# RWKV-7 attention before a mixture of experts: products over the head dimension issued for both head parities in turn

## The chip, the cores and the metric

The kernel runs on one core of one Trainium2 chip. The metric is the device time of one execution in microseconds (us). Three runs of the kernel before gave 2517.96, 2530.65 and 2545.3 us; the median is 2530.65 us.

The engines that matter here are TensorE (PE; its weight loads are listed apart as PEld), VectorE (DVE) and ScalarE (ACT), which empty PSUM, GpSimd (POOL), and SyncE (SP), which starts most transfers. Every matrix product is in float32. The profile shows one such product as two weight loads and two matmuls.

## The reference

The first part is a linear attention with a state per head, 4 batch rows, 8 heads, 768 steps, head dimension 40:

```
for t in range(S):
    y[:, :, t] = einsum('bhd,bhde->bhe', rt, state)
    Sa = einsum('bhde,bhe->bhd', state, at)
    state = state * wt[..., None, :] - einsum('bhd,bhe->bhde', Sa, bt)
    state = state + einsum('bhd,bhe->bhde', vt, kt)
```

Its output, as 3072 rows of 320, goes through a top-1 mixture of 8 experts (320 to 1024 to 320, a relu between), each row scaled by its gate weight.

## The kernel before, in words

The attention is cut into chunks of 128 steps: 6 chunks for each of 4 batch rows, 24 units, taken chunk by chunk (units 0 to 3 are the first chunk and have no incoming state). A unit holds all 8 heads as 4 head pairs. The even head of a pair (parity 0) has its 40 dimensions on partitions 0 to 39, the odd head (parity 1) on partitions 64 to 103; `rows(par)` is that slice. So a product over the head dimension reads 40 partitions of one half, and a product over time reads all 128.

Each unit is done by four functions.

- `prepare` loads the inputs, forms the running product of w, its reciprocal (DVE) and the scaled inputs, and transposes four tensors (`ps_nat`, 16 transposes).
- `systems` builds, for each parity, four masked 128x128 matrices per head by products over the head dimension (`ps_GT`, `ps_NT`, `ps_N`, `ps_AT`, line 177, 40 rows), and then squares the system matrix: 9 sets of four products over time (`ps_NT`, `ps_N`, line 177, 128 rows), emptied by ACT.
- `attend` solves the system for each parity: a right side (`ps_r`: for each head pair a product with the state, line 224, 40 rows, then one with `GT`, line 225, 128 rows), 8 sets of four products (`ps_q`, line 216), each set waiting for the DVE addition of the one before. Then come the transposes of the solution (`ps_uT`, line 246), the masked products `ps_ZT` (line 177, 40 rows), the output `ps_y` (for each head pair lines 263, 264 and 267: 40, 128 and 128 rows), the new state (`ps_s`, lines 273 and 274, written to one column half) and its transpose (`ps_st`, line 284).
- `route` computes the logits (`ps_xT`, `ps_lg`) and stores the gated rows.

The loop prepares unit u+1 and builds its systems, then attends to unit u, so the squaring of one unit and the chain of `ps_q` of another can share TensorE. PSUM has two rings: `big`, 5 buffers of 2 KB a partition, and `small`, 3. The order in each engine's queue is fixed when the program is built: a scheduler places the instructions, and every engine then works down its own list and waits where a result is missing.

The second part routes the rows and runs the experts; the change does not touch it.

Of the kernel before, what the change touches and what calls it, by code (L numbers as in the profile page):

```python
# [8 lines left out]
F32 = mybir.dt.float32  # L9
# [7 lines left out]
# Order of the six tensors in the packed attention input.  # L17
# [4 lines left out]
def kernel(  # L22
# [20 lines left out]
    N = B * S  # L43
# [10 lines left out]
    # The model dimension in contraction blocks.  # L54
# [3 lines left out]
    # Routing: NJ blocks of 128 rows for each expert, the rest in NX blocks shared by all.  # L58
# [50 lines left out]
    # Token numbers as float16 holds them: 1.. for the first half, -1.. for the second.  # L109
# [15 lines left out]
    with tc.tile_pool(name="ring", bufs=1) as ring, \  # L125
# [3 lines left out]
        # Head 2p+par has its dims at partitions par*64...; the partitions between hold harmless values.  # L129
# [24 lines left out]
        def prepare(u):  # L154
# [10 lines left out]
            # The same by time on the partitions.  # L165
# [18 lines left out]

        def systems(d):
            I = d["I"]
            for par in range(2):
                def of(n, par=par):
                    return lambda p: I[rows(par), n, p, :]

                def mat(t):
                    return lambda p: t[:, p, :]
# [14 lines left out]
        def attend(u, d):  # L207
# [10 lines left out]

            for par in range(2):
                rs = rows(par)  # L220
                q = small("ps_r")
                for p in range(NP):
                    if c:
                        nc.tensor.matmul(q[:, p, :], lhsT=I[rs, A, p, :], rhs=ST[rs, p, :], start=True, stop=False)  # L224
                    nc.tensor.matmul(  # L225
                        q[:, p, :], lhsT=d["GT", par][:, p, :], rhs=nV[:, p, par, :D], start=(c == 0), stop=True,
                    )
                X = sb.tile([C, NP, D], F32, name="X", bufs=6)
                nc.scalar.copy(X[:], q[:])
# [25 lines left out]
            for par in range(2):  # L255
                rs = rows(par)
                ZT = product(
                    lambda p: uT[rs, p, :], lambda p: I[rs, R, p, :], before, "ZT", 2,
                )
                q = small("ps_y")  # L260
                for p in range(NP):
                    if c:
                        nc.tensor.matmul(q[:, p, :], lhsT=I[rs, R, p, :], rhs=Sn[rs, p, :], start=True, stop=False)  # L263
# [6 lines left out]
                if c + 1 < NCH:  # L270
# [12 lines left out]
                    for p in range(NP):  # L283
                        nc.tensor.matmul(q[rs, p, :], lhsT=STn[rs, p, :], rhs=ident[rs, rs], start=True, stop=True)  # L284
# [285 lines left out]
```

## Time and profile before

| | |
|---|---|
| runs | 2517.96, 2530.65, 2545.3 us (median 2530.65) |
| profiled execution | span 2515.5 us, mean granted TensorE clock 0.716 |
| TensorE busy | 2373.8 us (94%), weight loads 2069.5 us (82%) |
| VectorE, ScalarE, GpSimd busy | 529.6 us, 415.7 us, 151.8 us |
| transfers | 59.58 MB, mean 24 GB/s |
| first part of the kernel (16 to 2135 us) | clock 0.98 up to 103 us, 0.72 up to 331 us, 0.66 up to 2051 us |
| experts (2200 to 2515 us) | clock 0.99 |

The page's busy times count an engine as busy while any of its instructions is under way. The granted clock of TensorE stands at one of two levels, 0.50 (1.2 GHz) or 1.00 (2.4 GHz); a figure between is a stretch with both. The time of the profiled execution is known by its span; what lies around the span is not listed, and the fastest of the three runs is 2.5 us above it.

### The profile page before, as it was taken

To read this page: it belongs to the slowest core of one execution; us is meant where nothing else is said; L and a number is where in the kernel's file an instruction comes from. 1 tells how busy PE (TensorE), PEld (TensorE's weight loads), DVE (VectorE), ACT (ScalarE), POOL (GpSimd) and SP (SyncE) were. 2 spreads that over 40 slices of the span, in tenths; PEclk is the share of its full clock that TensorE was granted. 3 is DMA by queue.
4 is the path that set the end of the run, shared out by engine and by line. 5 is a ranking of instruction groups with operands and counts; after the bars stand their busy time and mean duration, and the time that the engine had idled before them with its cause. 6 is when DMAs were issued, how large, how long until landed. Compare 5 with 4: busy or idle time off the path is not lost.

```text
span 2515.5 us, 29177 instructions
## 1 busy us (share of the span) xinstructions
PE 2373.8 (94%) x12916; PEld 2069.5 (82%) x12916; DVE 529.6 (21%) x1157; ACT 415.7 (17%) x849; POOL 151.8 (6%) x185
## 2 busy tenths in 40 slices
PE   6999999999999999999999999999999998699998
PEld 5999988998898898898899899899889887244544
DVE  2212222122122122122212112213112111311110
ACT  1312211221121121121121121111112110001010
POOL 4000000000000000000000000000000000311101
PEclk9877657766765766666676676676677665799999
DMA  1000000000000000000000000000000000522210
GB/s 48 19 9 11 19 19 16 4 19 19 1 19 19 3 17 19 10 10 19 16 3 19 16 4 19 19 1 19 19 1 19 3 1 3 155 93 85 86 51 16
DMA packets 20560, 59.58 MB, mean 24 GB/s; under 512 B 2893, under 2 KB 14159, under 8 KB 18512
## 3 DMA queue, kind: packets, MB, share of 16 engines
q1 hardware_dynamic: 16992, 48.50, 6.6%
q0 software_dynamic: 3072, 9.18, 1.2%
q8 instruction: 102, 1.67, 0.3%
q14 instruction: 26, 0.21, 0.0%
q10 hardware_dynamic: 368, 0.01, 0.0%
HBM read 49.82 MB, written 9.18 MB: 23 GB/s over the span
## 4 chain that ended last, share of the span: by engine, by line
PE 82%; issue 11%; DVE 3%; POOL 2%; ACT 1%; DMA 0%; POOLq 0%; DVEq 0%; ACTq 0%
PE ps_q L216 20%; PE ps_NT L177 14%; PE ps_N L177 11%; PE ps_y L264 4%; PE ps_ZT L177 4%; PE ps_y L267 4%; PE ps_y L263 3%; PE ps_nat L169 3%; PE ps_r L225 3%; PE ps_r L224 3%; PE ps_AT L177 3%; PE ps_GT L177 3%; DVE X L233 2%; POOL out_dram L493 1%; PE ps_st L284 1%
## 5 line engine op out<-in xcount | busy, mean ns | idle before, releaser
L216 PE MATMUL ps_q<-X,NT 128*128 128x40 f32 x2304 | 399.7, 332 | 52.7 <-DVE X L233 50.2
L216 PEld LDWEIGHTS ps_q<-X,NT 128*128 128x128 f32 x2304 | 378.2, 248 | 70.1 <-DVE X L233 65.7
L177 PE MATMUL ps_NT<-NT,N 128*128 128x128 f32 x1920 | 332.6, 326 | 1.3 <-ACT N L180 1.0
L177 PEld LDWEIGHTS ps_NT<-NT,N 128*128 128x128 f32 x1920 | 282.6, 226 | 13.2 <-issue 8.9
L177 PE MATMUL ps_N<-N,NT 128*128 128x128 f32 x1536 | 249.7, 317 | 0.0
L180 ACT COPY NT<-ps_NT 128x512 f32<-128x512 f32 x240 | 140.4, 585 | 584.9 <-PE ps_NT L177 584.9
L177 PEld LDWEIGHTS ps_N<-N,NT 128*128 128x128 f32 x1536 | 235.2, 234 | 0.0
L233 DVE TENSOR_TENSOR X<-ps_q,X 128x160 f32<-128x160 f32 x240 | 77.6, 323 | 574.9 <-PE ps_q L216 574.9
L474 PE MATMUL hp<-xgT,w 128*128 128x512 f32 (+1 forms) x384 | 190.9, 627 | 0.0
L474 PEld LDWEIGHTS hp<-xgT,w 128*128 128x128 f32 (+1 forms) x384 | 63.2, 189 | 122.4 <-issue 120.4
L216 PE MATMUL ps_q<-Z,NT 128*128 128x40 f32 x768 | 142.1, 348 | 20.5 <-DVE Z L242 20.5
L216 PEld LDWEIGHTS ps_q<-Z,NT 128*128 128x128 f32 x768 | 135.8, 266 | 27.7 <-DVE Z L242 27.7
L487 PE MATMUL zp<-w,h_sb 128*128 128x320 f32 x512 | 145.0, 433 | 0.0
L180 ACT COPY N<-ps_N 128x512 f32<-128x512 f32 x192 | 112.3, 585 | 107.9 <-PE ps_N L177 107.9
L264 PE MATMUL ps_y<-natK,AT 128*128 128x40 f32 x384 | 123.0, 420 | 0.0
L487 PEld LDWEIGHTS zp<-w,h_sb 128*128 128x128 f32 x512 | 94.6, 191 | 34.5 <-issue 0.8
L267 PE MATMUL ps_y<-natB,ZT 128*128 128x40 f32 x384 | 120.1, 415 | 0.0
L267 PEld LDWEIGHTS ps_y<-natB,ZT 128*128 128x128 f32 x384 | 101.9, 327 | 6.8 <-issue 4.3
L264 PEld LDWEIGHTS ps_y<-natK,AT 128*128 128x128 f32 x384 | 96.4, 311 | 13.3 <-issue 0.9
L177 PE MATMUL ps_ZT<-in,uT 40*128 40x128 f32 x384 | 101.0, 440 | 4.6 <-ACT uT L248 2.7
L263 PE MATMUL ps_y<-S,in 40*128 40x40 f32 x320 | 100.9, 414 | 0.0
L158 POOL MEMSET PT<- 128x4 f32 x24 | 2.5, 105 | 1573.8 <-DVE ST L279 1280.2
(150 smaller groups left out, 2384.4 us busy)
## 6 DMA issues: line engine op xcount, KB each, us to landing
in<-in_packed_dram SPq DMA_DIRECT2D x48, 480.0 KB
w<-in_moe_w_dram SPq DMA_DIRECT2D x8, 1280.0 KB
w<-in_moe_w_dram SPq DMA_DIRECT2D x8, 1024.0 KB
x_rows<-xs SPq DMA_DIRECT2D x24, 160.0 KB
w<-in_moe_w_dram SPq DMA_DIRECT2D x8, 256.0 KB
xg<-x_rows,g_idx POOLq DMA_INDIRECT x32
out_dram<-zo,s_idx POOLq DMA_INDIRECT x32
wg_sb<-in_moe_w_gate_dram ACTq DMA_DIRECT2D x2, 4.0 KB
```

What stands on the lines that cost most here:

```text
L169: nc.tensor.transpose(ps[:, p, :], src[:, p, :], ident[:])
L177: nc.tensor.matmul(ps[:, p, :], lhsT=lhs(p), rhs=rhs(p), start=True, stop=True)
L180: nc.scalar.copy(t[:], ps[:])
L216: nc.tensor.matmul(q[:, p, :], lhsT=m[:, p, :], rhs=x[:, p, :], start=True, stop=True)
L224: nc.tensor.matmul(q[:, p, :], lhsT=I[rs, A, p, :], rhs=ST[rs, p, :], start=True, stop=False)
L225: nc.tensor.matmul(q[:, p, :], lhsT=d["GT", par][:, p, :], rhs=nV[:, p, par, :D], start=(c == 0), stop=True,)
L233: nc.vector.tensor_tensor(Xn[:], q[:], X[:], op=ALU.add)
L263: nc.tensor.matmul(q[:, p, :], lhsT=I[rs, R, p, :], rhs=Sn[rs, p, :], start=True, stop=False)
L264: nc.tensor.matmul(q[:, p, :], lhsT=d["AT", par][:, p, :], rhs=nK[:, p, par, :D], start=(c == 0), stop=False,)
L267: nc.tensor.matmul(q[:, p, :], lhsT=ZT[:, p, :], rhs=nB[:, p, par, :D], start=False, stop=True)
L474: nc.tensor.matmul(hp[:, :cols], lhsT=g["w"][0][:dsz, db, fb * 128 : (fb + 1) * 128], rhs=g["xT"][:dsz, db, :cols], start=(db == 0), stop= ...
L487: nc.tensor.matmul(zp[:], lhsT=g["h"][:, fb, j * 128 : (j + 1) * 128], rhs=g["w"][1][:, fb, :], start=(fb == 0), stop=(fb == FB - 1),)
```

## The change

The four masked matrices of `systems` and the `ps_ZT` products are built by a new function, `twin`, which takes two PSUM buffers, one for each parity, and issues the products of the two parities in turn, pair by pair. All of `systems`' matrices of both parities are built before the squaring of either begins. The right side is made for both parities ahead of both chains: first the 8 products with the state, the parities in turn, then the 8 with `GT`. The new state is computed ahead of the output, with the parities in turn, and the output's 8 state products come as one group ahead of those with `AT` and `ZT`, which stay together by parity. No product is added or left out; the PSUM rings keep their sizes, and `ZT` has 4 buffers in place of 2.

```
+        def twin(lhs, rhs, mask, tag, bufs):
+            ps = [big(f"ps_{tag}") for _ in range(2)]
+            for p in range(NP):
+                for par in range(2):
+                    nc.tensor.matmul(ps[par][:, p, :], lhsT=lhs(par, p), rhs=rhs(par, p), start=True, stop=True)
+            ts = []
+            for par in range(2):
+                t = sb.tile([128, NP, 128], F32, name=tag, bufs=bufs)
+                nc.vector.tensor_tensor(t[:], ps[par][:], mask[:, None, :].to_broadcast([128, NP, 128]), op=ALU.mult)
+                ts.append(t)
+            return ts
...
+            d["GT"] = twin(of(K), of(A), before, "GT", 4)
+            NT0 = twin(of(B_), of(A), before, "NT0", 4)
+            N0 = twin(of(A), of(B_), after, "N", 4)
+            d["AT"] = twin(of(V), of(R), before, "AT", 4)
             for par in range(2):
-                d["GT", par] = product(of(K), of(A), before, "GT", 4)
-                NTk = product(of(B_), of(A), before, "NT0", 4)
-                Nk = product(of(A), of(B_), after, "N", 4)
-                d["AT", par] = product(of(V), of(R), before, "AT", 4)
+                NTk, Nk = NT0[par], N0[par]
...
+            qr = [small("ps_r") for _ in range(2)]
+            if c:
+                for p in range(NP):
+                    for par in range(2):
+                        rs = rows(par)
+                        nc.tensor.matmul(
+                            qr[par][:, p, :], lhsT=I[rs, A, p, :], rhs=ST[rs, p, :], start=(p == 0), stop=False,
+                            skip_group_check=True,
+                        )
+            for p in range(NP):
+                for par in range(2):
+                    nc.tensor.matmul(
+                        qr[par][:, p, :], lhsT=d["GT"][par][:, p, :], rhs=nV[:, p, par, :D],
+                        start=(c == 0 and p == 0), stop=True, skip_group_check=True,
+                    )
...
+            ZT = twin(lambda par, p: uT[rows(par), p, :], lambda par, p: I[rows(par), R, p, :], before, "ZT", 4)
...
+            qy = [small("ps_y") for _ in range(2)]
+            if c:
+                for p in range(NP):
+                    for par in range(2):
+                        rs = rows(par)
+                        nc.tensor.matmul(
+                            qy[par][:, p, :], lhsT=I[rs, R, p, :], rhs=Sn[rs, p, :], start=(p == 0), stop=False,
+                            skip_group_check=True,
+                        )
+            for par in range(2):
+                for p in range(NP):
+                    nc.tensor.matmul(
+                        qy[par][:, p, :], lhsT=d["AT"][par][:, p, :], rhs=nK[:, p, par, :D],
+                        start=(c == 0 and p == 0), stop=False, skip_group_check=True,
+                    )
+                    nc.tensor.matmul(
+                        qy[par][:, p, :], lhsT=ZT[par][:, p, :], rhs=nB[:, p, par, :D], start=False, stop=True,
+                        skip_group_check=True,
+                    )
```

The lists below are pieces of TensorE's queue in a unit of the middle of the kernel, one row for each run of equal products. `in_130` and `in_131` are input buffers of two successive units; names with a number are buffers.

First place: the start of `systems`. Before, the products of parity 0 alone:

```order
L177 MATMUL ps_GT<-in_131 128x128 x4
L177 MATMUL ps_NT_3587<-in_131 128x128 x4
L177 MATMUL ps_N<-in_131 128x128 x4
L177 MATMUL ps_AT<-in_131 128x128 x4
L177 MATMUL ps_NT_3608<-NT_3592,N 128x128 x4
L177 MATMUL ps_N<-N,NT_3592 128x128 x4
L216 MATMUL ps_q<-X,NT_3149 128x40 x4
```

With the change, in the same place:

```order
L190 MATMUL ps_GT<-in_131 128x128 x8
L190 MATMUL ps_NT_3587<-in_131 128x128
L190 MATMUL ps_NT_3588<-in_131 128x128
...
L190 MATMUL ps_N<-in_131 128x128 x8
L190 MATMUL ps_AT<-in_131 128x128 x8
L177 MATMUL ps_NT_3629<-NT_3597,N 128x128 x4
L177 MATMUL ps_N<-N,NT_3597 128x128 x4
L239 MATMUL ps_r<-ST_2055,in_130 128x40 x8
L245 MATMUL ps_r<-natV,GT 128x40
```

The rows with x8 alternate the parities as the `ps_NT` rows do. The four sets of parity 1, which stood between the squaring of parity 0 and that of parity 1, have moved up here, and `ps_r`, which stood ahead of the transposes and in the second squaring, has moved down.

Second place: the end of the squaring and the chain of `ps_q`. Before:

```order
L177 MATMUL ps_NT_3755<-NT_3746,N 128x128 x4
L216 MATMUL ps_q<-X,NT_3219 128x40 x4
L216 MATMUL ps_q<-X,NT_3240 128x40 x4
L216 MATMUL ps_q<-X,NT_3254 128x40 x4
L216 MATMUL ps_q<-X,NT_3268 128x40 x4
L216 MATMUL ps_q<-X,NT_3282 128x40 x4
L216 MATMUL ps_q<-X,NT_3296 128x40 x4
L216 MATMUL ps_q<-Z,NT_3296 128x40 x8
```

With the change:

```order
L177 MATMUL ps_NT_3748<-NT_3739,N 128x128 x4
L231 MATMUL ps_q<-Z,NT_3227 128x40 x8
L231 MATMUL ps_q<-X,NT_3136 128x40 x4
L231 MATMUL ps_q<-X,NT_3234 128x40 x4
L231 MATMUL ps_q<-X,NT_3248 128x40 x4
L231 MATMUL ps_q<-X,NT_3262 128x40 x4
L231 MATMUL ps_q<-X,NT_3276 128x40 x4
L231 MATMUL ps_q<-X,NT_3290 128x40 x4
L231 MATMUL ps_q<-Z,NT_3290 128x40 x8
```

Of the 16 `ps_q` sets of a unit, 8 stood behind the last squaring; now 10 do.

Third place: the output, in parity 0 before:

```order
L177 MATMUL ps_ZT<-in_130,uT 128x128 x3
L267 MATMUL ps_y<-natB,ZT 128x40
L263 MATMUL ps_y<-S_2059,in_130 128x40
L264 MATMUL ps_y<-natK,AT 128x40
L273 MATMUL ps_s<-natV,natK 40x40
L274 MATMUL ps_s<-u_145,natB 40x40
```

With the change:

```order
L190 MATMUL ps_ZT<-in_130,uT 128x128 x8
L302 MATMUL ps_st<-ident,ST_3895 40x40 x8
L310 MATMUL ps_y<-S_2056,in_130 128x40 x4
L316 MATMUL ps_y<-natK,AT 128x40
L310 MATMUL ps_y<-S_2056,in_130 128x40 x4
L320 MATMUL ps_y<-natB,ZT 128x40
L316 MATMUL ps_y<-natK,AT 128x40
```

The 40-row products stood singly between 128-row products, 8 times in a unit; now they stand in two groups of four, and the new state is finished ahead of them.

## Rows read from the trace of the kernel before

**Rows 1.** The page: span, and busy time with share and instructions of each engine.

```profile
span 2515.5 us, 29177 instructions
PE 2373.8 (94%) x12916; PEld 2069.5 (82%) x12916; DVE 529.6 (21%) x1157; ACT 415.7 (17%) x849; POOL 151.8 (6%) x185
```

**Rows 2.** The page: shares of the chain that ended last, by engine.

```profile
PE 82%; issue 11%; DVE 3%; POOL 2%; ACT 1%; DMA 0%; POOLq 0%; DVEq 0%; ACTq 0%
```

**Rows 3.** Timeline of TensorE: transposes of the solution, units 3 and 22.

```profile
330.78 1.12 PE L246 MATMUL ps_uT<-ident,u 128*128 128x128 f32 x4
...
2050.94 1.09 PE L246 MATMUL ps_uT<-ident,u 128*128 128x128 f32 x4
```

**Rows 4.** Windows, one unit: stretch, length, busy of PE, PEld, DVE, ACT, POOL, clock, DMA.

```profile
1325.69:1345.86 20.17, 20.05 (x104) 17.64 (x102) 4.31 (x12) 0.87 (x2) 0.11 (x1) 0.50 0.12 32
1345.86:1357.76 11.90, 11.90 (x52) 10.86 (x50) 5.13 (x9) 3.69 (x11) 2.44 (x2) 0.50 0.10 30
1357.76:1364.88 7.12, 7.12 (x33) 6.90 (x32) 2.08 (x3) 0.58 (x1) 0.00 (x0) 0.50 0.06 23
1364.88:1378.12 13.24, 13.24 (x105) 13.12 (x104) 1.99 (x5) 4.68 (x8) 0.00 (x0) 0.90 0.00 1
1378.12:1382.49 4.37, 4.37 (x34) 4.14 (x33) 2.08 (x3) 0.58 (x1) 0.00 (x0) 0.85 0.00 0
1382.49:1400.36 17.87, 17.87 (x114) 17.49 (x114) 1.67 (x4) 4.97 (x9) 0.00 (x0) 0.75 0.00 1
1400.36:1415.88 15.52, 12.53 (x67) 11.51 (x65) 2.27 (x7) 0.58 (x1) 0.00 (x0) 0.65 0.00 1
1415.88:1417.85 1.97, 1.97 (x15) 1.74 (x14) 0.32 (x1) 0.00 (x0) 0.00 (x0) 0.50 0.00 0
```

**Rows 5.** Windows: the clock around the products of parity 1, same columns.

```profile
1368.20:1378.12 9.92, 9.92 (x88) 9.80 (x87) 1.30 (x4) 4.09 (x7) 0.00 (x0) 1.00 0.01 2
1378.12:1381.20 3.08, 3.08 (x28) 3.08 (x28) 1.41 (x3) 0.58 (x1) 0.00 (x0) 1.00 0.00 0
1381.40:1391.30 9.90, 9.90 (x48) 9.68 (x47) 1.48 (x3) 1.75 (x3) 0.00 (x0) 0.50 0.01 2
```

**Rows 6.** Timeline (start, length, engine, line, tiles, count, [idle before]): 40-row sets, 1.2 GHz.

```profile
1359.63 1.91 PE L177 MATMUL ps_NT<-in 40*128 40x128 f32 x8
1361.33 1.91 PE L177 MATMUL ps_N<-in 40*128 40x128 f32 x8
```

**Rows 7.** Timeline of TensorE: two successive squarings at 2.4 GHz, a `ps_q` between them.

```profile
1371.58 1.16 PE L177 MATMUL ps_NT<-NT,N 128*128 128x128 f32 x8
...
1374.31 1.16 PE L177 MATMUL ps_NT<-NT,N 128*128 128x128 f32 x8
```

**Rows 8.** Timeline of TensorE: 40-row and 128-row products of the output in turn.

```profile
1332.32 0.65 PE L263 MATMUL ps_y<-S,in 40*128 40x40 f32 x2
1332.89 0.65 PE L264 MATMUL ps_y<-natK,AT 128*128 128x40 f32 x2
...
1333.90 0.65 PE L263 MATMUL ps_y<-S,in 40*128 40x40 f32 x2
```

**Rows 9.** Timeline of TensorE: one of the serial `ps_q` sets at 1.2 GHz.

```profile
1409.33 1.93 PE L216 MATMUL ps_q<-X,NT 128*128 128x40 f32 x8 [0.42 <-DVE X L233]
```

**Rows 10.** Timeline of TensorE: `ps_ZT` of one parity, and in the last unit of both.

```profile
1327.48 2.07 PE L177 MATMUL ps_ZT<-in,uT 40*128 40x128 f32 x8
...
2119.56 3.10 PE L177 MATMUL ps_ZT<-in,uT 40*128 40x128 f32 x16 [0.67 <-ACT uT L248]
```

**Rows 11.** Windows of `ps_ZT` alone in the last unit: PE, PEld, DVE, clock, DMA.

```profile
2119.80:2120.40 0.60, 0.60 (x4) 0.60 (x5) 0.00 (x0) 0.50 0.00 0
2120.80:2121.20 0.40, 0.40 (x6) 0.40 (x7) 0.00 (x0) 0.50 0.00 0
```

**Rows 12.** Groups by line: the masked eviction, and one of the two state products.

```profile
L182 DVE TENSOR_TENSOR GT<-ps_GT,before 128x512 f32<-128x512 f32 x48 | 33.2, 692 | 117.0 <-PE ps_GT L177 116.9
L273 PE MATMUL ps_s<-natV,natK 128*40 128x40 f32 x320 | 47.3, 269 | 0.0
```

More of the change, by code (lines that the diff above doesn't have):

```diff
@@ L217, in apply @@
                 return q
-            for par in range(2):
[L220 to L227, printed above, removed]
+            qr = [small("ps_r") for _ in range(2)]
[13 more added lines that the diff above has]
+                    )
+            for par in range(2):
                 X = sb.tile([C, NP, D], F32, name="X", bufs=6)
-                nc.scalar.copy(X[:], q[:])
+                nc.scalar.copy(X[:], qr[par][:])
                 for i in range(LEVELS):
@@ L254, in attend @@
                 st[b] = (STn, Snn)
[L255 to L260, printed above, removed]
-                for p in range(NP):
-                    if c:
-                        nc.tensor.matmul(q[:, p, :], lhsT=I[rs, R, p, :], rhs=Sn[rs, p, :], start=True, stop=False)
-                    nc.tensor.matmul(
-                        q[:, p, :], lhsT=d["AT", par][:, p, :], rhs=nK[:, p, par, :D], start=(c == 0), stop=False,
-                    )
-                    nc.tensor.matmul(q[:, p, :], lhsT=ZT[:, p, :], rhs=nB[:, p, par, :D], start=False, stop=True)
-                nc.vector.tensor_tensor(x[:, :, par, :], q[:], nP[:, :, par, :D], op=ALU.mult)
-                if c + 1 < NCH:
-                    q = small("ps_s")
-                    for p in range(NP):
-                        nc.tensor.matmul(q[rs, p, :], lhsT=nK[:, p, par, :D], rhs=nV[:, p, par, :D], start=True, stop=False)
-                        nc.tensor.matmul(q[rs, p, :], lhsT=nB[:, p, par, :D], rhs=U[:, p, par, :D], start=False, stop=True)
+            ZT = twin(lambda par, p: uT[rows(par), p, :], lambda par, p: I[rows(par), R, p, :], before, "ZT", 4)
+            if c + 1 < NCH:
+                q = small("ps_s")
+                for p in range(NP):
+                    for par in range(2):
+                        nc.tensor.matmul(
+                            q[rows(par), p, :], lhsT=nK[:, p, par, :D], rhs=nV[:, p, par, :D], start=True, stop=False,
+                        )
+                    for par in range(2):
+                        nc.tensor.matmul(
+                            q[rows(par), p, :], lhsT=nB[:, p, par, :D], rhs=U[:, p, par, :D], start=False, stop=True,
+                        )
+                for par in range(2):
+                    rs = rows(par)
                     PC = d["PT"][rs, :, C : C + 1].to_broadcast([D, NP, D])
@@ L281, in attend @@
                         nc.vector.tensor_tensor(STn[rs], q[rs], PC, op=ALU.mult)
[L282 to L285 removed]
+                qq = [small("ps_st") for _ in range(2)]
+                for p in range(NP):
+                    for par in range(2):
+                        rs = rows(par)
+                        nc.tensor.matmul(qq[par][rs, p, :], lhsT=STn[rs, p, :], rhs=ident[rs, rs], start=True, stop=True)
+                for par in range(2):
+                    nc.scalar.copy(Snn[rows(par)], qq[par][rows(par)])
+            qy = [small("ps_y") for _ in range(2)]
+            if c:
+                for p in range(NP):
+                    for par in range(2):
+                        rs = rows(par)
+                        nc.tensor.matmul(
+                            qy[par][:, p, :], lhsT=I[rs, R, p, :], rhs=Sn[rs, p, :], start=(p == 0), stop=False,
+                            skip_group_check=True,
+                        )
+            for par in range(2):
+                for p in range(NP):
+                    nc.tensor.matmul(
+                        qy[par][:, p, :], lhsT=d["AT"][par][:, p, :], rhs=nK[:, p, par, :D],
+                        start=(c == 0 and p == 0), stop=False, skip_group_check=True,
+                    )
+                    nc.tensor.matmul(
+                        qy[par][:, p, :], lhsT=ZT[par][:, p, :], rhs=nB[:, p, par, :D], start=False, stop=True,
+                        skip_group_check=True,
+                    )
+                nc.vector.tensor_tensor(x[:, :, par, :], qy[par][:], nP[:, :, par, :D], op=ALU.mult)
             return x
```

10 lines of the change are left out of this document (4 added, 6 removed).

## The prediction

> **What bounds the kernel now.** I read the page's busy line first: TensorE is busy for 2373.8 of 2515.5 us, no other engine above 21% [rows 1], and 82% of the chain that ended last is TensorE's [rows 2]. So the question is what TensorE's own list costs. I then looked for a stretch that repeats. The transposes `ps_uT` come once a unit; from unit 3 to unit 22 there are 19 intervals in 1720.16 us, 90.53 us each [rows 3]. This is where the time is, and one of these units, 92.16 us long, is cut into eight stretches in [rows 4]: end of `attend` (20.17, its first 1.97 us in the last row), transposes with the first right side (11.90), the four sets of parity 0 (7.12), first squaring (13.24), four sets of parity 1 (4.37), second squaring (17.87), serial chain (15.52). PE is busy throughout, except in the chain. What the reader is to see beside it is the clock: 1.2 GHz in most of these rows, 2.4 GHz only inside the squarings. It rises in the first squaring, whose mean of 0.90 over 13.24 us means 2.6 us at 0.50 [rows 4]; stays at 1.00 to 1381.20, through 3 us of the 40-row sets of parity 1; and is 0.50 from 1381.40 to 1391.30 [rows 5], although PE never paused. Later it falls again in the chain (mean 0.65), where PE waits.
>
> **Prices.** A set of four 40-row products takes 1.70 us at 1.2 GHz (start to start, [rows 6]). In the squarings, `ps_NT`, `ps_N` and `ps_q` follow in 2.73 us at 2.4 GHz [rows 7], 0.91 us a set, whatever the moving width. A 40-row product followed by a 128-row one takes 0.57 us [rows 8] against 1.70/4 = 0.43 in a run of equals, so a change of shape costs 0.14. A serial `ps_q` set takes 1.93 + 0.42 = 2.35 us [rows 9].
>
> **What a pair on two halves costs.** Before, the parities never alternate, but in the last unit the two `ps_ZT` sets stand next to each other: 16 matmuls in 3.10 us, where one set of 8 takes 2.07 [rows 10]. While one half works alone, 4 matmuls and 5 loads touch a stretch of 0.60 us; where the halves meet, 6 and 7 touch one of only 0.40 [rows 11]. So loads and matmuls of the two halves do run at once, at the seam. The bounds for a fully alternated pair are then half of two products, and two products in full. I take half, since the overlap in the seam is that dense: 0.85 us a set at 1.2 GHz in place of 1.70.
>
> **The change, part by part, for a unit with a state.**
>
> 1. *Systems.* 32 products in one block, after the transposes, at 1.2 GHz: 8 sets x 0.85 + 0.15 entry = 7.0 us, for 7.12 + 4.37 before. DVE empties 8 tiles at 0.69 us, 5.5 us [rows 12], beside it, inside the 7.0.
>
> 2. *Transposes and routing.* `ps_r` (4 pairs at 2 x 0.57, less the seam: 4.5) and one `ps_q` set (1.8 with its interruption) leave this stretch: 11.90 - 6.3 = 5.6. They were cover: the first `ps_xT` now follows the last `ps_y` directly and waits for the DVE product, which I put at 0.5 us, like the chain's 0.42 wait. 6.1. The reciprocal is not exposed, since in DVE's list it now precedes the output's products.
>
> 3. *Squarings.* 18 sets, 6 `ps_q` sets, the 8 `GT` products (2 sets) and the 8 paired state products (1 set): 27 sets in one stretch, with nothing of parity 1 in between. The low stretch at 1381.40 to 1391.30 goes with the block that stood before it. I take one low start, 3 us as in the first squaring: 1.8 sets at 1.70. The other 25.2 sets x 0.91 = 22.9, three changes of shape 0.4. 26.4, for 13.24 + 17.87 plus what step 2 sent here.
>
> 4. *Serial chain.* 10 sets stand behind the last squaring in place of 8: 15.52 + 2 x 2.35 = 20.2. This is the change's own cost; parity 0's chain begins later, since the right side has moved down past the transposes and the products of the next unit.
>
> 5. *End of `attend`.* 20.17 + 1.97 = 22.1. The eight triples of `ps_y` took 1.58 us each [rows 8], 12.6; now 2 paired sets 0.85, 4 sets 1.70 and four changes: 1.7 + 6.8 + 0.6 = 9.1, 3.5 less. `ps_ZT` halves, 1.7 less. The state products, alternating on column halves, no row shows: `ps_s` is booked with 2 x 47.3 us over 20 units [rows 12], 4.7 a unit, so the gain lies between nothing and 2.4; nearest are the row halves, but these are short, so 1.0. 15.9 left.
>
> Sum: 7.0 + 6.1 + 26.4 + 20.2 + 15.9 = 75.6, for 90.53: 14.9 less, times 19 = 283 us. Outside these: three intervals without a state have only steps 1, 3 and part of 5, and ran at a better clock; about half, 7 each, 21. The head, some 4, and the last unit without cover, two ends of `attend` and 16 `ps_r` pairs, some 12. Together 320: 2515.5 becomes 2195. The median of the runs is 15 us above the profiled span, so the **forecast is 2210 us**.
>
> SP's and POOL's lists keep their order, so no transfer moves. PSUM is not short: a `twin` holds two of five `big` buffers, and DVE frees one every 0.69 us while PE fills one every 0.85.
>
> **Rivals.**
>
> *The clock rises earlier.* The twin block may itself bring 2.4 GHz. Against it: the 40-row block of 7.12 us ran at 0.50 from end to end [rows 4]. For it: now twice the rows work at a time. Then step 1 is bound by DVE, 5.5 + 0.2, and step 3 has no low start, 24.9: 2.8 us less a unit, 2155 us. The Trainium skill, "TensorE: Matmul & The Clock Gate", Part 1 (The HAM clock gate), says that sustained matmul activity releases the clock and idleness takes it; by that rule alone this case would be the rule, and the fall at 1381 in [rows 5], without any idleness, would not happen. The measurement decides, so it stays a rival. The skill's "TensorEngine Tiling (Array Packing)", section PSUM Bottleneck, says that tiling speeds up TensorE but not the emptying of PSUM; that is the 5.5 us here, which binds in this case alone.
>
> *Half the overlap.* The pairs cost 0.75 instead of 0.5, as the queue may not reach far enough past the second load of a product. Then 3.4 us more in step 1, 0.9 in `ps_ZT`, 1.3 in the state products, 0.5 in `ps_s`: 6.1 a unit, 2325 us.
>
> *No overlap.* The alternation is only another order: 12.2 us a unit more than the forecast, 87.8, and little is left: some 2470 us. [rows 10] speaks against it.
>
> *Slower: the clock does not come back in the squarings.* The place is step 3, where `ps_r` now breaks the first squarings up. With x us of it at 1.2 GHz, a unit takes 49.2 + 0.4 + 0.91 x (27 - x/1.70) + x = 74.2 + 0.465 x; it is slower than 90.53 from x = 35 on. If the whole stretch of 46 us is low, and the 2.4 GHz start of the chain is lost too (two sets, 0.85 each), a unit takes 97.3, 6.8 more than before: 19 x 6.8 - 37 = 92 more, 2620 us. Against it: in both squarings before, the clock was back within 10 us [rows 5]. With 10 us low at the start, 3.3 us more a unit, the time is 2272, which belongs to the forecast's own range.
>
> **How the numbers follow.** Chances: forecast 0.62 (2210, its own range 2140 to 2280), earlier clock 0.15 (2155), half overlap 0.12 (2325), no overlap 0.06 (2470), slower 0.05 (2620). The range 2110 to 2340 takes in the first three cases with the bounds of step 5 and of the units without a state, and leaves out the last two and the tails. The three runs span 27 us, so about 1% is what can be told from no change. Faster by over 1%: the first three cases and most of the fourth, 0.93; same 0.03; slower 0.04.
>
> **What would show it.** Right: intervals of `ps_uT` near 75 us; the twin block in 7 us with loads of two halves side by side; a clock that rises once a unit, at the start of the squarings, and stays up to the chain; 9 waits for DVE in the chain. Wrong: a twin block of 13.9 us; a wait of PE for DVE's masked evictions or for a `big` buffer; a clock at 0.50 through the squarings; a TensorE wait ahead of the transposes that need the scaled inputs, where the right side's products are no longer there to hide POOL.

## The result, and the profile after

The changed kernel takes 2159.16 us (median of 4 runs, 2158.44 to 2161.42). The kernel before, beside it, takes 2526.18 us (median of 4). The ratio is 0.8536, with a 95% interval of 0.8501 to 0.8571: 14.6% less time. The forecast was 2210 us, with a range of 2110 to 2340. In what follows a median is of all runs of a kernel, while a ratio leaves out runs over 1.5% above the kernel's fastest, which are one of the four of `e8_route_late` and two of the four of `e12_mixed_end`.

In the changed kernel's line numbers, L190 is `twin`, L177 the squarings, L231 `ps_q`, L239 and L245 the two halves of the right side, L268 `ps_uT`, L282 and L286 `ps_s`, L335 `ps_xT`. The page, its busy line and its shares of the chain, for [rows 1, 2]:

```profile
span 2156.7 us, 29213 instructions
PE 1991.0 (92%) x12916; PEld 1728.3 (80%) x12916; DVE 518.7 (24%) x1157; ACT 417.4 (19%) x849; POOL 151.1 (7%) x185
PE 65%; issue 13%; DVE 4%; POOL 2%; DMA 0%; ACT 0%; POOLq 0%; DVEq 0%
```

The number of TensorE instructions is the same, 12916, and the span is 358.8 us shorter. TensorE is still the bound. The mean granted clock went from 0.716 to 0.751. As the clock has two levels, that is 1429 us at 1.2 GHz before and 1074 after (twice what the mean lacks to 1, times the span), and 1087 and 1083 us at 2.4 GHz. All that was saved is time at the low clock.

The solution's transposes in units 3 and 22, for [rows 3]:

```profile
309.24 1.12 PE L268 MATMUL ps_uT<-ident,u 128*128 128x128 f32 x4
...
1702.86 1.11 PE L268 MATMUL ps_uT<-ident,u 128*128 128x128 f32 x4
```

That is 73.35 us an interval in place of 90.53: 326 us of the 358.8. The 19 intervals are of two kinds: 11 last 74.7 to 75.6 us, 8 last 68.3 to 72.3 (the last two of these, 68.3 us each, belong to units that compute no new state). One of the longer kind, for [rows 4], is cut into the prediction's steps: end of `attend`, transposes, twin block, squarings, chain (length, then busy time of PE, PEld, DVE, ACT and POOL, clock, DMA share, GB/s):

```profile
1346.56:1362.71 16.15, 15.73 (x111) 14.64 (x111) 8.02 (x14) 1.16 (x3) 2.55 (x3) 0.50 0.25 61
1362.71:1368.31 5.60, 5.60 (x26) 4.88 (x26) 0.87 (x3) 2.45 (x6) 0.00 (x0) 0.50 0.01 3
1368.31:1375.44 7.13, 7.13 (x66) 6.91 (x65) 4.18 (x8) 1.44 (x4) 0.00 (x0) 0.50 0.06 23
1375.44:1401.62 26.18, 26.18 (x226) 25.91 (x225) 3.23 (x8) 10.45 (x19) 0.00 (x0) 0.95 0.01 1
1401.62:1421.91 20.29, 16.89 (x89) 15.55 (x87) 3.24 (x10) 0.59 (x1) 0.00 (x0) 0.59 0.00 1
```

The clock in the last two of these stretches, for [rows 5], and then in a unit of the shorter kind:

```profile
1375.44:1378.10 2.66, 2.66 (x15) 2.66 (x14) 1.29 (x2) 0.55 (x1) 0.00 (x0) 0.54 0.00 0
1378.10:1401.62 23.52, 23.52 (x213) 23.25 (x213) 1.95 (x6) 9.90 (x19) 0.00 (x0) 1.00 0.01 1
1401.62:1405.20 3.58, 2.96 (x26) 2.73 (x24) 0.74 (x3) 0.59 (x1) 0.00 (x0) 1.00 0.00 0
1405.20:1421.91 16.71, 13.93 (x63) 12.82 (x63) 2.50 (x8) 0.00 (x0) 0.00 (x0) 0.50 0.01 1
...
771.00:777.10 6.10, 5.68 (x28) 5.17 (x27) 0.92 (x2) 2.33 (x6) 0.00 (x0) 0.50 0.01 3
777.10:782.10 5.00, 4.93 (x68) 4.36 (x68) 3.67 (x10) 1.56 (x5) 0.00 (x0) 1.00 0.09 33
```

In this unit of the longer kind the clock rises 2.7 us into the squarings (2.2 to 3.1 us in the eleven), stays up to the chain, and falls there. In this unit of the shorter kind it rises 0.6 us ahead of the twin block, in the last transposes. TensorE's timeline shows what that does to the block; the first two rows are sets of the longer kind, for [rows 6], the others of the shorter:

```profile
1370.18 1.92 PE L190 MATMUL ps_NT<-in 40*128 40x128 f32 x16
1371.88 1.92 PE L190 MATMUL ps_N<-in 40*128 40x128 f32 x16
...
777.34 0.44 PE L169 MATMUL ps_nat<-ident,PT 128*128 128x128 f32 x2
777.71 1.16 PE L190 MATMUL ps_GT<-in 40*128 40x128 f32 x16
...
782.11 1.16 PE L177 MATMUL ps_NT<-NT,N 128*128 128x128 f32 x8
```

At 1.2 GHz, sixteen matmuls (eight products, both parities) come 1.70 us after one another, the time that [rows 6] shows for eight matmuls. At 2.4 GHz the whole block takes 782.11 - 777.71 = 4.40 us.

`ps_ZT` of both parities and the next tile's first product, for [rows 10], and a serial set, for [rows 9]:

```profile
1348.69 2.08 PE L190 MATMUL ps_ZT<-in,uT 40*128 40x128 f32 x16
1350.70 0.76 PE L302 MATMUL ps_st<-ident,ST 40*40 40x40 f32 x16
...
1407.83 1.93 PE L231 MATMUL ps_q<-X,NT 128*128 128x40 f32 x8 [0.42 <-DVE X L255]
```

The output's state products, for [rows 8], in the same unit:

```profile
1351.38 1.92 PE L310 MATMUL ps_y<-S,in 40*128 40x40 f32 x8
1353.24 0.65 PE L316 MATMUL ps_y<-natK,AT 128*128 128x40 f32 x2
1353.81 1.93 PE L310 MATMUL ps_y<-S,in 40*128 40x40 f32 x8
```

The source issues these eight products with the parities in turn, too, but in the queue they stand as four, a product with `AT`, and four. Each four take 1.86 us (1353.24 - 1351.38), the price of four products that do not overlap (1.70 us and the change of shape), where the twin block puts eight into 1.70. So the overlap that the change was written for is missing here, in all 16 units that read a state and compute a new one; in the last four, which compute none, the eight take 2.57 us.

Groups by line, busy us and mean ns; the last two are for [rows 12]:

```profile
L190 PE MATMUL ps_ZT<-in,uT 40*128 40x128 f32 x384 | 49.0, 431 | 0.0
L190 PE MATMUL ps_AT<-in 40*128 40x128 f32 x384 | 42.2, 362 | 0.8 <-DVE NT L194 0.6
L190 PE MATMUL ps_GT<-in 40*128 40x128 f32 x384 | 41.3, 378 | 0.0
...
L282 PE MATMUL ps_s<-natV,natK 128*40 128x40 f32 x320 | 27.1, 269 | 0.0
L286 PE MATMUL ps_s<-u,natB 128*40 128x40 f32 x320 | 29.3, 266 | 0.0
```

The mean of one `ps_s` matmul is unchanged at 269 ns, but the group's busy time fell from 47.3 to 27.1 us: the matmuls on the two column halves overlap too. The two groups overlap each other as well, before and after, so their times must not be added: TensorE is busy with `ps_s` as a whole for 55.6 us before and 32.4 after, 1.2 us less in each of 20 units.

### The profile page after: what moved, and what is told of

It reads as the page before. It is cut to its first block, busy times and chain, and to the rows that moved or that the text cites. A ratio compares the mean times of both kernels' runs of the same rounds, so it can differ in the third digit from the quotient of the medians.

```text
span 2156.7 us, 29213 instructions
## 1 busy us (share of the span) xinstructions
PE 1991.0 (92%) x12916; PEld 1728.3 (80%) x12916; DVE 518.7 (24%) x1157; ACT 417.4 (19%) x849; POOL 151.1 (7%) x185
## 4 chain that ended last, share of the span: by engine, by line
PE 65%; issue 13%; DVE 4%; POOL 2%; DMA 0%; ACT 0%; POOLq 0%; DVEq 0%
PE ps_q L231 20%; PE ps_NT L177 9%; PE ps_N L177 6%; PE ps_y L320 3%; PE ps_y L316 3%; PE ps_nat L169 3%; PE ps_y L310 3%; PE ps_ZT L190 2%; PE ps_r L245 2%; DVE X L255 2%; POOL out_dram L532 1%; PE ps_GT L190 1%; PE ps_AT L190 1%; PE ps_N L190 1%; PE hp L513 1%
## 5 line engine op out<-in xcount | busy, mean ns | idle before, releaser
L231 PE MATMUL ps_q<-X,NT 128*128 128x40 f32 x2304 | 397.1, 332 | 51.8 <-DVE X L255 51.6
L231 PEld LDWEIGHTS ps_q<-X,NT 128*128 128x128 f32 x2304 | 375.7, 247 | 69.0 <-DVE X L255 68.6
L177 PE MATMUL ps_NT<-NT,N 128*128 128x128 f32 x1920 | 285.4, 296 | 2.1 <-DVE N L194 1.0
L177 PEld LDWEIGHTS ps_NT<-NT,N 128*128 128x128 f32 x1920 | 243.7, 200 | 10.3 <-DVE N L194 3.3
L177 PE MATMUL ps_N<-N,NT 128*128 128x128 f32 x1536 | 211.1, 282 | 0.0
L177 PEld LDWEIGHTS ps_N<-N,NT 128*128 128x128 f32 x1536 | 196.3, 200 | 0.0
L231 PE MATMUL ps_q<-Z,NT 128*128 128x40 f32 x768 | 141.7, 347 | 28.0 <-DVE Z L264 28.0
L231 PEld LDWEIGHTS ps_q<-Z,NT 128*128 128x128 f32 x768 | 132.2, 260 | 37.3 <-DVE Z L264 36.7
L270 ACT COPY uT<-ps_uT 128x512 f32<-128x512 f32 x24 | 14.1, 586 | 486.0 <-PE ps_uT L268 486.0
L316 PEld LDWEIGHTS ps_y<-natK,AT 128*128 128x128 f32 x384 | 102.5, 328 | 2.0
L169 PE MATMUL ps_nat<-ident,in 128*128 128x128 f32 x288 | 76.0, 420 | 24.6 <-DMA in<-in_packed_dram 16.5
```

The lines of the kernel that those rows point to most:

```text
L169: nc.tensor.transpose(ps[:, p, :], src[:, p, :], ident[:])
L177: nc.tensor.matmul(ps[:, p, :], lhsT=lhs(p), rhs=rhs(p), start=True, stop=True)
L231: nc.tensor.matmul(q[:, p, :], lhsT=m[:, p, :], rhs=x[:, p, :], start=True, stop=True)
L316: nc.tensor.matmul(qy[par][:, p, :], lhsT=d["AT"][par][:, p, :], rhs=nK[:, p, par, :D], start=(c == 0 and p == 0), stop=False, skip_group_ ...
```

## The experiments

Three theories were tested: (a) the gain is the overlap of successive products on different row halves of the array; (b) what is left of the change's loss is the longer serial chain; (c) the forecast's error is the clock, which in some units rises ahead of the twin block. Rivals: for (a), that the grouping alone gives the gain; for (b), that the chain is covered. The kernel before took 2524 to 2525 us beside all of these. "Interval" is the mean of the 19 `ps_uT` intervals.

| kernel | median us | ratio to before, 95% interval | interval, us | clock |
|---|---|---|---|---|
| after | 2159.16 | 0.8536 (0.8501 to 0.8571) | 73.35 | 0.751 |
| e1_seams | 2221.67 | 0.8798 (0.8753 to 0.8844) | 76.49 | 0.743 |
| e2_blocks | 2358.52 | 0.9331 (0.9290 to 0.9372) | 82.39 | 0.722 |
| e14_one_half | 2250.24 | 0.8914 (0.8873 to 0.8954) | 78.33 | 0.733 |
| e3_systems_only | 2343.00 | 0.9270 (0.9230 to 0.9310) | 82.77 | 0.734 |
| e4_attend_only | 2323.36 | 0.9194 (0.9150 to 0.9239) | 79.82 | 0.734 |
| e6_two_chains | 1868.74 | 0.7385 (0.7357 to 0.7413) | 60.14 | 0.843 |
| e10_logits_late | 2086.62 | 0.8251 (0.8222 to 0.8280) | 70.94 | 0.783 |
| e11_both | 1857.10 | 0.7340 (0.7312 to 0.7368) | 61.06 | 0.861 |
| e8_route_late | 2051.48 | 0.8088 (0.8022 to 0.8154) | 69.71 | 0.792 |
| e12_mixed_end | 1859.14 | 0.7302 (0.7259 to 0.7345) | 61.12 | 0.839 |
| e13_mixed_y | 1889.51 | 0.7479 (0.7447 to 0.7511) | 61.96 | 0.835 |

**The same queue on one row half.**

In this list and in those below, `-` is the changed kernel unless the text says otherwise, and `...` stands for lines left out.

```
-            d["AT"] = twin(of(V), of(R), before, "AT", 4)
+            d["AT"] = twin(lambda par, p: I[rows(0), V, p, :], lambda par, p: I[rows(0), R, p, :], before, "AT", 4)
...
-            ZT = twin(lambda par, p: uT[rows(par), p, :], lambda par, p: I[rows(par), R, p, :], before, "ZT", 4)
+            ZT = twin(lambda par, p: uT[rows(0), p, :], lambda par, p: I[rows(0), R, p, :], before, "ZT", 4)
```

> The changed kernel, with ps_AT and ps_ZT of both parities reading parity 0's rows (so AT and ZT of parity 1 hold parity 0's products; they go into the output only). TensorE's queue is the same, row by row; only the row half of parity 1's operands differs. Theory: the halved time comes from successive products standing on different row halves. Then the eight products of ps_AT take 3.4 us at 1.2 GHz instead of 1.7 to 1.8, and those of ps_ZT 3.4 instead of 2.0: 3.1 us a unit, by 24 units 74 us, a little less where the clock is up: 2215 to 2235 us, and more if the later squarings then bring the clock back later. Rival: the gain comes from the grouping (eight products in a row, two PSUM buffers, fewer changes between 40 and 128 rows); then the time stays at 2159 us.

Measured: 2250.24 us, 91 more than the changed kernel. Its groups by line, beside those of the changed kernel above, and three windows: a `ps_ZT`, and the start of the squarings in two long intervals.

```profile
L190 PE MATMUL ps_ZT<-in,uT 40*128 40x128 f32 x384 | 89.0, 421 | 0.0
L190 PE MATMUL ps_AT<-in 40*128 40x128 f32 x384 | 71.3, 354 | 0.9 <-DVE NT L194 0.6
L190 PE MATMUL ps_GT<-in 40*128 40x128 f32 x384 | 40.2, 370 | 0.0
...
1395.58:1399.29 3.71, 3.71 (x18) 3.48 (x16) 2.66 (x8) 0.00 (x0) 0.11 (x1) 0.50 0.00 0
798.51:807.33 8.82, 8.82 (x48) 8.52 (x48) 0.96 (x2) 1.76 (x3) 0.00 (x0) 0.50 0.01 2
1498.88:1514.40 15.52, 15.52 (x82) 15.21 (x82) 4.04 (x4) 3.22 (x6) 1.34 (x2) 0.52 0.00 1
```

`ps_ZT` goes from 49.0 to 89.0 us and `ps_AT` from 42.2 to 71.3, while `ps_GT`, whose operands were left alone, stays. The mean of one matmul is the same to 3%, so what the row halves change is how many run at once. TensorE's list is the same, so grouping alone cannot give that part: (a) holds, and the rival is out for these tiles. (`AT` and `ZT` of parity 1 then hold parity 0's products, which changes values and not the work.) The two tiles cost 69 us of the 91. Behind the last `ps_ZT` both kernels take 390 us, so the rest is not the second part's. It goes with the clock, whose late return the expectation named without a size: the clock comes back 8.7 to 9.0 us into the squarings in nine of the 12 long intervals of this kernel, and 15 us in the other three (the last row, 0.52), where the changed kernel has 2.2 to 3.1; the time at 1.2 GHz is 1200 us in place of 1074. The Trainium skill, "TensorEngine Tiling (Array Packing)", section Tiling Modes, says that tiles on different parts of the array load weights and multiply independently; the trace agrees, with 49.0 against 89.0 us.

**The order inside the twin block.** `e1_seams` exchanges the two loops of `twin`, so the halves meet only where four products of one follow four of the other. `e2_blocks` also writes out the four matrices of parity 0 and then those of parity 1, ahead of both squarings.

```
             for p in range(NP):                  # e1
                 for par in range(2):
becomes
             for par in range(2):
                 for p in range(NP):
...
+            for par in range(2):                 # e2, besides; at(n) slices rows(par) of tensor n
+                d["GT"].append(product(at(K), at(A), before, "GT", 4))
+                NT0.append(product(at(B_), at(A), before, "NT0", 4))
+                N0.append(product(at(A), at(B_), after, "N", 4))
+                d["AT"].append(product(at(V), at(R), before, "AT", 4))
```

> Only the two loops inside twin are exchanged: the four products of parity 0, then the four of parity 1, everything else as in the changed kernel. Theory (two row halves work at once, and only neighbours of different parity overlap): the halves meet only at the seams between sets; a seam saved 0.4 us in the last unit of the kernel before, so the block of eight sets takes 13.6 - 7 x 0.4 = 10.8 us at 1.2 GHz in place of 7.1, the ps_ZT pair 3.0 in place of 2.0: 4.7 us a unit, about 2255 us. Rival (the gain is from where the sets stand and from the grouping, not from the overlap): 2160 us.

> As e1_seams, and the four matrices of parity 0 are built before the four of parity 1, so one seam is left in the block; it still stands ahead of both squarings. Theory: the block takes 13.6 - 0.4 = 13.2 us at 1.2 GHz, 6.1 more; ps_ZT 1.0 more; and the units in which the clock has risen in the transposes lose it again in the block: 7 to 9.5 us a unit, 2295 to 2340 us. Rival (order, not overlap): 2160 us.

Measured: 2221.67 and 2358.52 us, 63 and 199 more than the changed kernel. Windows: the 32 products of `systems` and a `ps_ZT` of `e1_seams`, then the 32 products of `e2_blocks`, all at 1.2 GHz:

```profile
1186.42:1195.56 9.14, 9.14 (x65) 8.92 (x64) 5.06 (x9) 1.44 (x4) 0.00 (x0) 0.50 0.05 18
1165.78:1168.80 3.02, 3.02 (x18) 2.80 (x16) 2.19 (x6) 0.00 (x0) 0.10 (x1) 0.50 0.00 0
...
1434.12:1447.38 13.26, 13.26 (x65) 13.04 (x64) 5.06 (x9) 1.44 (x4) 0.00 (x0) 0.50 0.03 12
```

The same 32 products take 7.13 us alternating by pair, 9.14 by four, 13.26 by sixteen. For `e1_seams`, 2.0 in the block and 1.0 in `ps_ZT` are 3.0 us a unit; the mean interval grew by 3.1. That the two agree so well is partly chance, since the intervals run from 66.9 to 84.5 us with the clock, and in nine of the 19 the block runs at 2.4 GHz, where it takes 4.96 us against the changed kernel's 4.40. The expectation of 2255 us, 96 more, was too high: a seam saves 0.64 us here ((13.6 - 9.14) / 7), not 0.4, and the units at 2.4 GHz were not in it. For `e2_blocks` the block is as expected, 13.26 us, but the time lies 18 us above the expected 2295 to 2340.

`e2_blocks` also bounds what (a) explains. With hardly any overlap left in the twin products it is still 166 us faster than the kernel before. So 199 of the 367 us hang on the order within the twin products; the rest belongs to what `e2_blocks` and the changed kernel share (the place of the sets ahead of the squarings, the paired `ps_r` and `ps_s`, the grouped output), and no run separates these.

**Each half of the change alone.** `e3_systems_only` is the kernel before with the new `systems`; `e4_attend_only` is the changed kernel with the old one.

```
-            d["GT"] = twin(of(K), of(A), before, "GT", 4)   # e4: taken out; e3: the only part put in
-            NT0 = twin(of(B_), of(A), before, "NT0", 4)
...
```

> The kernel before with the new systems alone (alternating parities, all eight sets ahead of the squarings); attend as before. Theory: 7.1 us for 7.1 + 4.4, and one low-clock stretch of 10 us (4.5 us) less between the squarings: 8 to 9 us a unit, about 2360 us. Rival (the larger part is the grouping in attend): 2450 us or more.

> The complement: systems as before, with the sets of parity 1 between the squarings and no alternation there; attend, ps_ZT, ps_s and ps_y as in the changed kernel. Theory: what e3 gains is missing here, so about 2526 - 367 + 166 = 2325 us, with the clock falling again after the sets of parity 1. If the two parts help or hinder each other through the clock, the gains of e3 and e4 do not add up to 367 us.

Measured: 2343.00 and 2323.36 us, close to both theories (2360 and 2325), and 182 and 201 us less than before, 383 together, where both at once give 367. The parts very nearly add; neither is the whole.

**The serial chain.** `e6_two_chains` advances the chains of the two parities in turn.

```
-            for par in range(2):
-                ...
-                for i in range(LEVELS):
-                    q = apply(d["NT", par][i], X)
+            for i in range(LEVELS):
+                for par in range(2):
+                    q = apply(d["NT", par][i], X[par])
```

> The changed kernel, with the two parities' chains of ps_q advanced in turn (level by level, parity 0 then parity 1) instead of one chain after the other; no product added or left out. Theory: step 4 of the prediction, ten serial sets behind the last squaring, 19.8 us a unit at 1.2 GHz with 0.42 us of waiting for VectorE in a set, is what is left of the change's loss; TensorE's queue now has only four sets of the Z rounds behind the last squaring, and the other parity's set covers the addition. Six sets move into the squarings (0.91 us each at 2.4 GHz, 5.5 us), four stay (1.7 us each at 1.2 GHz, 6.8 us): 12.3 for 19.8 us, 7.5 us by 19 intervals is 143: about 2015 us; about 1965 us if the clock stays up through the last four sets. Rival: the chain's waits are covered elsewhere, and the time stays within 1% of 2159 us.

Measured: 1868.74 us, 290 less than the changed kernel and below both values of the theory. TensorE's timeline at the end of a chain, then windows of one unit: squarings and chain, the tiles behind them, and a low stretch.

```profile
1061.32 1.14 PE L177 MATMUL ps_NT<-NT,N 128*128 128x128 f32 x8
1062.29 3.66 PE L231 MATMUL ps_q<-Z,NT 128*128 128x40 f32 x32
...
1034.40:1066.37 31.97, 31.83 (x295) 31.62 (x294) 5.20 (x16) 10.48 (x19) 0.00 (x0) 1.00 0.01 2
1066.40:1070.70 4.30, 4.14 (x71) 3.50 (x71) 2.41 (x8) 1.16 (x3) 0.10 (x1) 1.00 0.01 2
1009.70:1033.50 23.80, 23.38 (x138) 22.21 (x138) 11.30 (x18) 3.94 (x11) 2.44 (x2) 0.50 0.17 49
```

Four sets stand behind the last squaring, and none waits. From the last squaring's end to `ps_uT` it is 4.1 us (1066.37 - 1062.29) where the changed kernel takes 20.29, and the squarings that took up the other six sets are 4.8 us longer (31.0 from 1031.34 to 1062.29, for 26.18). What the expectation had too small is the clock: it also stays up through the chain's end, `ps_uT`, `ps_s` and `ps_ZT`. (b) holds in so far as the chain was the largest cost that remained; its waits went together with the low clock, and this run does not tell the two apart. It moves all the serial sets, too, and not only the two that the change added, so the 290 us are not the size of the change's loss.

**The clock ahead of the twin block.** `e10_logits_late` moves the logits product of a unit behind the next unit's chain, so the transposes run unbroken; `e11_both` joins this to the chains in turn; `e8_route_late` has the chains in turn and all of `route` moved, the transposes `ps_xT` too.

```
-            x = attend(u, d)
-            route(u, x)
+            x = attend(u, d, pend)       # e10, e11: logits(*pend) runs behind the chain
+            pend = route(u, x)           # e8: attend itself calls route(u - 1, x_last) there
```

> The changed kernel with the logits product ps_lg (and the row scaling behind it) deferred until after the next unit's chain, so that the transposes ps_xT and ps_nat run without a break right ahead of the twin block; the queue also takes ps_r and the first ps_q ahead of them and leaves six instead of ten serial sets behind the last squaring. Theory of the rival that held in a third of the units (the clock rises ahead of the twin block when the transposes run unbroken): it now rises there in every unit, the twin block takes about 4.5 instead of 7.1 us and the squarings have no low start (3.4 us of low clock a unit are gone in the 14 units that have it now); with four serial sets less (1.98 us each, against 0.91 us within the squarings: 4.3 us a unit) about 2035 us. If the clock does not rise there: the serial sets alone, about 2110 us (4.3 us by 19 is 82, less some of it lost to other waits).

> The two edits together: the parities' chains in turn and the logits deferred. If the two gains are of different stretches (serial sets, and the low clock of the twin block) they add: about 1900 us. If they are the same gain (both shorten the serial end behind the squarings), about 1965 to 2015 us, what the chains in turn give alone.

> The parities' chains in turn, and the whole of route (the transposes ps_xT, the logits, the store) of a unit done inside the next unit's attend, behind its chain, instead of at its own end. Only the 16 transposes ps_nat then stand ahead of the twin block, not 19. If what raises the clock ahead of the twin block is an unbroken run of transposes, and 16 are enough: within 2% of the kernel with only the logits deferred. If three more are needed: the twin block stays at 1.2 GHz, 7.1 us, and the time is about 50 us above that kernel's.

Measured: 2086.62, 1857.10 and 2051.48 us. Timeline of TensorE in `e10_logits_late` ahead of the transposes, then windows of its twin block and of that of `e8_route_late`:

```profile
1143.19 1.93 PE L239 MATMUL ps_r<-ST,in 40*128 40x40 f32 x8
1145.05 1.93 PE L245 MATMUL ps_r<-natV,GT 128*128 128x40 f32 x8
1147.41 1.93 PE L239 MATMUL ps_r<-ST,in 40*128 40x40 f32 x8 [0.44 <-ACT X L251]
...
1156.74:1161.07 4.33, 4.29 (x65) 3.94 (x64) 3.14 (x6) 0.61 (x2) 0.00 (x0) 1.00 0.00 0
...
1014.29:1021.42 7.13, 7.13 (x66) 6.91 (x65) 3.87 (x6) 0.58 (x1) 0.00 (x0) 0.50 0.00 0
```

The clock did rise ahead of the twin block, which took 4.33 us, in 12 of the 19 intervals; in the other 7 it rose within the block's first 1.4 us. But the time is neither of the two expected. The right side moved with the rest, to 1.2 GHz, and `ps_r` lost its pairing: four state products of one parity in 1.86 us, then the products with `GT`, then the other parity. In the changed kernel `ps_r` runs paired inside the squarings (eight state products in 1.02 us). So the twin block and the shorter chain gave, and the right side with its first set, 9.5 us at the low clock (1143.19 to 1152.70), took most of it back: the interval is 2.4 us shorter than the changed kernel's. In `e11_both` the interval is 61.06 us, no better than with the chains in turn alone; its 12 us less come from outside the 19 intervals. So the two gains do not add, although the time is below both values expected, because the chains in turn alone already were. In `e8_route_late` the twin block stayed at 0.50 in 17 of 19 intervals, as the second branch said, but the time is some 190 us above `e11_both`, not 50. More than the block moved: the low stretch of a unit is 37.5 us long, in `e11_both` 20.5.

```profile
916.68:954.22 37.54, 36.78 (x206) 35.37 (x204) 11.77 (x18) 4.08 (x9) 2.55 (x3) 0.50 0.11 27
...
818.88:839.36 20.48, 19.72 (x91) 19.22 (x91) 4.72 (x8) 1.87 (x6) 1.27 (x1) 0.50 0.16 43
```

Half of the 17 us between them is about the 8.6 us by which the mean intervals differ. As a test of what raises the clock ahead of the block, the run is inconclusive.

**The fall of the clock at the end of `attend`.** `e12_mixed_end` and `e13_mixed_y` start from the chains in turn. The list gives the order of the statements, not the code.

```
-            ZT = twin(...); ps_s; ps_st; ps_y: S (both parities); ps_y by parity: AT, ZT    # the chains in turn
+            ps_y: per pair S, S, AT, AT; ZT = twin(...); ps_s; ps_y: ZT; ps_st              # e12
+            ps_s; ZT = twin(...); ps_y: per pair S, S, AT, AT; ps_st; ps_y: ZT              # e13
```

> The kernel with the two chains in turn, with the end of attend written in another order: the output's products with the state and with AT first, in turn by head pair, then ZT, then the new state ps_s, then the products with ZT, and ps_st last. TensorE's queue puts state and AT products among the last squarings, and no longer has ps_ZT, ps_st and the state products of ps_y (48 products over 40 rows) in one group. In the kernel with the two chains in turn the clock falls there, in 17 of 19 intervals, and is low for 23.9 us of an interval's 61.3 us. Theory: it is that unbroken group over 40 rows that lets the clock fall; without it the clock stays at 2.4 GHz, the 23.9 us become 12, an interval about 49.4 us, and the time about 1640 us; up to 1750 us if it still falls in half of the intervals. Rival: the clock falls in the end of attend in whatever order (the waits for uT and x, or the output's products themselves): within 2% of 1869 us.

> The same, but only the AT products of the output are moved: they alternate by head pair with its state products, behind ZT, and ps_st goes behind them; ps_s stays ahead of ZT. ps_s, half of the state products and ZT still stand close together (about 3 us at 2.4 GHz, with ps_uT within). Theory (an unbroken group over 40 rows lets the clock fall): better than 1869 us, and not as good as the other order, 1680 to 1800 us. Rival: within 2% of 1869 us.

Measured: 1859.14 us (1835.0 to 1874.62; 1841.5 without the two longer runs) and 1889.51. Both lie within 2% of 1868.74, so the rival holds, and my theory, by which the time would have been 1640 to 1750 and 1680 to 1800 us, fell. Windows of the profiled execution of `e12_mixed_end`, which took 1870.2 us at a mean clock of 0.839 (the two shorter runs, at 0.856 and 0.862, left no trace, so how much of the loss below they have is not shown): a stretch of squarings, one round of it, and the end of `attend` behind.

```profile
969.08:999.96 30.88, 30.88 (x146) 30.88 (x145) 3.88 (x10) 5.26 (x9) 0.00 (x0) 0.50 0.01 1
979.48:986.31 6.83, 6.83 (x34) 6.83 (x33) 0.65 (x2) 1.17 (x2) 0.00 (x0) 0.50 0.00 1
1001.70:1025.50 23.80, 23.61 (x250) 22.36 (x249) 7.80 (x19) 6.76 (x14) 1.29 (x2) 1.00 0.14 40
```

In the last row the clock does stay up through `ps_ZT`, `ps_s` and the output, as the theory said. But it falls a little later, at the right side, and in intervals like this one four rounds of squaring and `ps_q` run at 0.50 with TensorE busy in every one of 30.88 us. The intervals scatter from 51 to 74 us. In this execution, what was won at the end of `attend` was lost in the squarings. What sets the clock there stays open.

## Why the prediction was right, step by step

**Mechanism.** Right in steps 1 to 4 of the longer kind of unit; in step 5 only the sum is right. Together the steps take 75.35 us against the forecast 75.6.

| step | forecast | longer kind | shorter kind (756.34 to 827.25) |
|---|---|---|---|
| 1 twin block | 7.0 | 7.13 | 4.40 |
| 2 transposes and routing | 6.1 | 5.60 | 5.21 |
| 3 squarings | 26.4 | 26.18 | 25.04 |
| 4 chain | 20.2 | 20.29 | 20.10 |
| 5 end of `attend` | 15.9 | 16.15 | 16.16 |

Step 1 took half for a pair, from the density at a seam of two sets [rows 11]; 1.70 us for eight products confirms it, and the queue on one half shows that it is the halves. The wait ahead of `ps_xT`, 0.5 in step 2, is there with 0.42 us, but stands at the end of step 5's row. Step 4 has eight of the nine waits that were foreseen, of 0.41 to 0.49 us each.

Step 5 is right by luck. Its term of 1.7 us for the output's state products, as two paired sets, failed: they did not overlap and took 1.86 us each, 2.0 us more a unit. What made up for it was sized too low or not in the sum: `ps_ZT` saved 2.2 us and not 1.7 ((101.0 - 49.0) / 24), and the transposes of the state `ps_st`, which the sum left as they were, overlap too and saved 0.8 (30.7 us busy before, 14.9 after, in 20 units). Besides, 0.5 us of `ps_s` now runs ahead of `ps_uT` (1421.42 to 1421.91) and counts in step 4's row. The groups before and after:

```profile
L177 PE MATMUL ps_ZT<-in,uT 40*128 40x128 f32 x384 | 101.0, 440 | 4.6 <-ACT uT L248 2.7
L284 PE MATMUL ps_st<-ident,ST 40*40 40x40 f32 x320 | 30.7, 265 | 1.6 <-DVE ST L281 1.6
...
L302 PE MATMUL ps_st<-ident,ST 40*40 40x40 f32 x320 | 14.9, 263 | 0.0
```

The bounds of 0 to 2.4 us for `ps_s`, taken from 2 x 47.3 us, were too wide, since its two groups overlap each other; the 1.0 chosen between them is near the 1.2 measured.

**What was mis-sized.** The term of the sum that failed is the clock in steps 1 and 3: "at 1.2 GHz" for the block in every unit. In 8 of 19 intervals the clock was up ahead of the block, and these are 5.0 us shorter than the forecast's (mean 70.6). That is 40 us of the 43 by which 19 x 73.35 stays under 19 x 75.6. Not all of it is the clock: the last two of the eight have no new state, and their end of `attend` takes 12.09 us in place of 16.15, which the forecast's 19 equal intervals had left out.

```profile
1566.33:1578.42 12.09, 10.90 (x55) 9.97 (x54) 1.94 (x4) 0.59 (x1) 0.00 (x0) 0.50 0.29 81
```

These are 8 us; the clock has the other 32. So the rival of the earlier clock was not an alternative to the forecast; both occur in turn in one execution, and why the clock rises early in some units and not in others stays open. The rival's own price was wrong too: it had the block bound by VectorE at 5.7 us, and it took 4.40, since the emptying of the last tiles runs on beside the first squarings (`AT` is done at 783.84, 1.7 us after the block). That the measured 2159 us lies next to the rival's 2155 is therefore chance.

**Smaller terms.** Outside the 19 intervals it is 32.3 us (358.8 - 326.5) for 37, 5 too many. The 15 us added for the median over the profiled span was wrong by 12.5: the median now lies 2.5 us above it (2159.16 - 2156.7). Together 43 - 5 + 12.5 = 51 us, the whole of the forecast's miss.

**Rivals.** Half the overlap and no overlap are out by the block's 7.13 us (`e2_blocks`, with one seam left, measures 13.26). The slower rival did not come here, where the clock was back 2.7 us into the squarings. But a clock that stays low in the squarings exists: 8.7 to 15 us of them in the kernel on one half, and over 30 us in `e12_mixed_end`. Half the overlap is out for the twin block only; the output's state products had none.

## What to carry to other kernels

Where products fill at most half of the rows (or columns), issue those of the two halves in turn, product by product: here eight such products then took the time of four, and every step back to blocks cost what its seams lost (at 1.2 GHz; at 2.4 GHz in turn by four cost only 4.96 for 4.40 us). Read the order in the queue that comes out, and not in the source: the output's state products are written in turn and did not overlap. Then look at what the new order leaves in series behind it: advancing the two chains in turn gave another 290 us here. Price each stretch at both levels of the clock, unit by unit, since the level there can change from one round of a loop to the next.

## What was not expected of the hardware

- With one queue, and the same work per product, 40-row products on one half in place of two cost their own 69 us and 22 us more, with a clock that in long intervals came back 8.7 to 15 instead of 2.2 to 3.1 us into the squarings.
- At 2.4 GHz the paired 40-row block keeps the clock (1.00 through 4.40 us), where four sets on one half were followed by a fall before [rows 5]. In turn by four (`e1_seams`) it stays up too, in nine of nine blocks; in `e2_blocks` it rose ahead of the block in 12 of 19 intervals and fell again within it.
- The Trainium skill, "TensorE: Matmul & The Clock Gate", Part 1 (The HAM clock gate), says that sustained matmul activity releases the clock. The rise in the unbroken transposes of `e10_logits_late` agrees with it; the 30.88 us at 0.50 with TensorE busy throughout in `e12_mixed_end` do not, and the measurement decides.
- The four best kernels, 1857 to 1890 us, differ from one another by less than the runs of a single one of them: `e12_mixed_end` took 1835.0 us at a mean clock of 0.862 and 1874.62 at 0.838.
